# Attention with a gated MLP on one core: layernorm rstd of three row chunks by a power on GpSimd

## The chip, the cores and the metric

One core of one Trainium2 chip runs the whole kernel in one launch. Its engines are TensorE (PE in the profile, its weight loads PEld), VectorE (DVE), ScalarE (ACT), GpSimd (POOL) and SyncE (SP, which only issues DMAs here). They run side by side and wait for each other on semaphores; each executes its own instructions in order. The metric is the time of one execution in device microseconds, the median of the runs.

## The reference

The input x is 2048 rows of 448 numbers in bf16. A layernorm without weights feeds two branches whose product is added to x.

```python
def _layernorm(x, axis=-1, eps=1e-5):
    m = jnp.mean(x, axis=axis, keepdims=True)
    v = jnp.var(x, axis=axis, keepdims=True)
    return (x - m) / jnp.sqrt(v + eps)
...
    # branch A: H = 16 heads of Dh = 28
    qkv = (x @ wqkv).reshape(B, S, 3, H, Dh)...
    p = _softmax(einsum("bhqd,bhkd->bhqk", q, k) * Dh ** -0.5)
    s = einsum("bhqk,bhkd->bhqd", p, v).reshape(B, S, D) @ wo
    # branch B: F = 1792
    g = silu(gelu(x @ w1 + b1) @ w2 + b2)
...
    xn = _layernorm(x)
    return x + s * g
```

The number 1 / sqrt(v + eps) of each row is called rstd below.

## The kernel before

**Chunks and blocks.** The 2048 rows are four chunks c of 512 rows, each of four tiles t of 128 rows. The 16 heads are four groups g of four heads. One block b of attention is one group with one chunk of queries, 16 blocks in all, b = 4g + c. Within a block the scores of 16 key tiles and four heads are made 512 queries wide: 64 steps m. The scores of two steps (first block) or three (later) form a unit; the exponentials of a unit are one ACT instruction (L1038), numbered from 0 here. The scores come from PE (L1011) into a ring of PSUM banks. Since a step's key tile is its number over four, the first block meets the keys of chunk 1 at exponential 8, those of chunk 2 at exponential 16 and those of chunk 3 at exponential 24. Some steps, a fixed list, have their exponential on DVE instead (L1065 to L1096). The products with the values (L1137) follow on PE.

**Layernorm.** p_ln makes each chunk's mean and variance on DVE (L606, L612, into mv), for chunks 0 and 1 in two halves of two tiles, for chunks 2 and 3 four tiles at once. p_ln2 then makes rstd: on ACT a Ln of the variance with eps as bias (L620, into lnv) and an Exp with scale -0.5 (L622, into rstd). For chunk 0 DVE normalizes (L633). For chunks 1 to 3 POOL negates the mean (L627, nm) and normalizes each tile (L637). So before the change each half of chunk 1, and chunk 2 and chunk 3, has two small ACT instructions.

**From there to the scores.** PE transposes the normalized tiles (L651; chunk 0 L744), DVE copies them out (L662, into xnT), PE projects keys (L671) and DVE evicts them (L682, kT); the values go by L876 and L886, the queries by L671, L852, a square on POOL (L857), a sum on PE (L859) and L862.

**POOL's other early work.** It makes the constants (L496 to L534), two memsets of the value pads (L540, L541), and after the last chunk's layernorm the squares and relayouts of the query and key weights (L702, L692) and a memset of wo (L588). The 16 loads of wo on SP's queue wait for that memset; the norms (L804) wait for the squares.

**What else is named.** The first layer of branch B goes by L916 and L929. One Gelu per chunk (L941) runs on ACT in one stretch once all of them are done, between two loads of activation tables. The second layer is L959 (14 matmuls for one tile, two per task) and L964, and the silu a tanh on ACT (L973). The output is a matmul (L1226), a product and a sum (L1235, L1237) and a DMA.

**What sets the order.** The Python program works the order out when it builds the kernel. Every piece of work is a generator that yields tasks; a task has an engine, the tokens it reads and writes, a planned duration and a priority (`_Task(E, fn, reads, writes, dur, lat, prio)`). The loop in `run` takes, again and again, the task with the earliest planned start; among tasks of that engine that could start within 0.1 of it, the one with the smallest priority number goes first. It then books the task's planned duration. The planned durations are the program's own figures and not measurements. A task that reads what the one before it on its engine wrote waits for that engine's own semaphore (on all engines but PE), and its planned start is at least 0.07 later. So the booked order of every engine follows from planned starts, and the chip then executes that order, each engine in its own.

Of the kernel before, what the change touches and what calls it, by code (L numbers as in the profile page):

```python
# [7 lines left out]
ACTF = mybir.ActivationFunctionType  # L8
ALU = mybir.AluOpType
ET = mybir.EngineType  # L10

PE, ACT, DVE, POOL, SP = ET.PE, ET.Activation, ET.DVE, ET.Pool, ET.SP
# [55 lines left out]
LN_EPS = 1e-5  # L68
# [28 lines left out]
class _Kernel:  # L97
# [19 lines left out]
    def sb(self, name, shape, dtype=dt.bfloat16):  # L117
        return self.es.enter_context(self.nc.sbuf_tensor(name, shape, dtype))
# [143 lines left out]
    def alloc(self):  # L262
        nc = self.nc
        f32, bf = dt.float32, dt.bfloat16
        sb = self.sb
# [35 lines left out]
        self.rhi = sb("rhi", [128, 16, 32], bf)  # L301
        self.rlo = sb("rlo", [128, 16, 32], bf)
        self.dum = sb("dum", [128, 1], f32)
        self.epsc = sb("epsc", [128, 1], f32)
        w1f = self.w1[:, :, :].rearrange("p k f -> p (k f)")
        self.fsb = w1f[:, 0:3584].rearrange("p (b t d) -> p b t d", b=2, t=4)
# [159 lines left out]
    def constants(self):  # L466
        K = self
        e = self.emit

        def f(eng):  # L470
            eng.memset(K.epsc[:, :], LN_EPS)
            eng.memset(K.dum[:, :], 1.0)
            eng.memset(K.ones[:, :], 1.0)
            eng.memset(K.E_sb[:, :, :], 0.0)
            eng.memset(K.stg[64:128, 3, :, :, :], 0.0)
            pad = lambda w: w.rearrange("p k (h e) -> p (k h) e", e=32)[:, :, DH:32]
            eng.memset(pad(K.wq[:, :, :]), 0.0)
            eng.memset(pad(K.wk[:, :, :]), 0.0)
            eng.memset(pad(K.wsq), 0.0)
            return eng.memset(K.xn[:, :, :, D:512], 0.0)  # L480
        e(DVE, f, writes=[K.b_pads], dur=1.6)

        def late_pads():
            yield ("until", lambda: K.b_xnT[0][1].tw is not None)

            def f(eng):
                eng.memset(K.wv[64:128, 3, :], 0.0)
                eng.memset(K.wv[0:64, 3, D:WS], 0.0)
                return eng.memset(K.wv[:, 0:3, D:WS], 0.0)
            yield _Task(DVE, f, [], [K.b_wvpad], 0.4, 0.05, 1)  # L490
            yield ("until", lambda: K.ln_done == 2 * C)
            yield _Task(DVE, lambda eng: eng.memset(K.w1[64:128, 3, :], 0.0), [], [K.b_w1pad], 0.8, 0.05, 4)
        K.spawn(late_pads(), 3)

        def f(eng):
            eng.iota(K.iota_p[:, :], [[0, 1]], base=0, channel_multiplier=1, allow_small_or_imprecise_dtypes=True)  # L496
            return eng.iota(K.iota_f[:, :], [[1, 128]], base=0, channel_multiplier=0, allow_small_or_imprecise_dtypes=True)
        io = _Buf()
        e(POOL, f, writes=[io], dur=0.4)

        def f(eng):
            return eng.tensor_scalar(K.ident[:, :], K.iota_f[:, :], K.iota_p[:, 0:1], None, op0=ALU.is_equal)
        e(POOL, f, reads=[io], writes=[K.b_id], dur=0.6)
        ec, tc = _Buf(), _Buf()
        e(POOL, lambda eng: eng.tensor_copy(K.ecol[:, 0:1], K.iota_p[:, :]), reads=[io], writes=[ec], dur=0.2)
        for thr in (32.0, 64.0, 96.0):
            e(POOL, lambda eng, thr=thr: eng.tensor_scalar(K.tcol[:, :], K.iota_p[:, :], thr, 32.0,
                                                           op0=ALU.is_ge, op1=ALU.mult), reads=[io], writes=[tc], dur=0.3)
            e(POOL, lambda eng: eng.tensor_tensor(K.ecol[:, 0:1], K.ecol[:, 0:1], K.tcol[:, :], ALU.subtract),
              reads=[ec, tc], writes=[ec], dur=0.3)  # L510

        def f(eng):
            eng.tensor_single_scalar(K.ecol[:, 1:2], K.ecol[:, 0:1], 28.0, ALU.is_lt)
            eng.tensor_scalar(K.ecol[:, 2:3], K.ecol[:, 0:1], 28.0, -1.0, op0=ALU.is_equal, op1=ALU.mult)
            return eng.tensor_tensor(K.ecol[:, 3:4], K.iota_p[:, :], K.ecol[:, 0:1], ALU.subtract)
        e(POOL, f, reads=[ec, io], writes=[K.b_cols], dur=0.8)
        e(POOL, lambda eng: eng.tensor_scalar(K.tcol[:, :], K.ecol[:, 3:4], 28.0, None, op0=ALU.add),
          reads=[K.b_cols], writes=[tc], dur=0.3)
        hm = _Buf()

        def f(eng):
            return eng.tensor_scalar(K.ecol[:, 0:1], K.ecol[:, 1:2], 0.5, None, op0=ALU.mult)
        e(POOL, f, reads=[K.b_cols], writes=[hm], dur=0.3)

        def f(eng):
            return eng.tensor_scalar(K.bsel[:, :], K.iota_f[:, :], K.tcol[:, 0:1], K.ecol[:, 0:1],
                                     op0=ALU.is_equal, op1=ALU.mult)
        e(POOL, f, reads=[tc, hm, io], writes=[K.b_bsel], dur=0.8)

        def f(eng):  # L530
            return eng.tensor_copy(K.sel[:, :], K.ident[:, :].rearrange("p (j e) -> p j e", e=32)[:, :, DH])
        e(POOL, f, reads=[K.b_id], writes=[K.b_bsel], dur=0.2)
        selb = K.selb[:, :].rearrange("p (j e) -> p j e", e=32)
        e(POOL, lambda eng: eng.tensor_copy(selb, K.sel[:, :, None].to_broadcast([128, 4, 32])), reads=[K.b_bsel],  # L534
          writes=[K.b_selb], dur=0.3)
        K.b_hf[1][0].r.append(K.b_bsel.w)

        def vpads():
            yield ("until", lambda: K.ready(K.b_xn[0], -0.1))
            yield _Task(POOL, lambda eng: eng.memset(K.vaug[:, :, :, DH:DH + 1], 2.0), K.b_xn[0], [K.b_vpad0], 1.2, 0.05, 2)  # L540
            yield _Task(POOL, lambda eng: eng.memset(K.vaug[:, :, :, DH + 1:32], 0.0), [K.b_vpad0], [K.b_vpad], 1.2, 0.05, 2)  # L541
        K.spawn(vpads(), 3)
        self.prog[ACT].append(lambda eng: eng.preload_act_table_set("natural_log_exp_and_others"))
        self.tE[ACT] = 2.1
# [72 lines left out]
    def p_ln2(self, c, h, ts):  # L617
        K = self
        sl = slice(4 * c + ts[0], 4 * c + ts[-1] + 1)
        yield _Task(ACT, lambda eng: eng.activation(K.lnv[:, sl], K.mv[:, sl, 1], ACTF.Ln, bias=K.epsc[:, 0:1]),  # L620
                    [K.b_mv[c][h], K.b_pads], [K.b_ln[c][h]], 0.3, 0.0, 2 if c else 0)
        yield _Task(ACT, lambda eng: eng.activation(K.rstd[:, sl], K.lnv[:, sl], ACTF.Exp, scale=-0.5),  # L622
                    [K.b_ln[c][h]], [K.b_rs[c][h]], 0.2, 0.0, 2 if c else 0)
        if len(ts) == 4:
            K.b_rs[c][1] = K.b_rs[c][0]
        if c > 0:
            yield _Task(POOL, lambda eng: eng.tensor_scalar(K.nm[:, sl], K.mv[:, sl, 0], -1.0, None, op0=ALU.mult),  # L627
                        [K.b_mv[c][h]], [K.b_nm[c][h]], 0.22, 0.05, c)
        for t in ts:
            i = 4 * c + t  # L630
            rd = [K.b_x0[h] if c == 0 else K.b_x[c], K.b_mv[c][h], K.b_rs[c][h], K.b_pads]
            if c == 0:
                yield _Task(DVE, lambda eng, i=i, t=t: eng.tensor_scalar(  # L633
                    K.xn[:, c % 3, t, 0:D], K.x_sb[:, c, t, :], K.mv[:, i, 0:1], K.rstd[:, i:i + 1],
                    op0=ALU.subtract, op1=ALU.mult), rd, [K.b_xn[c % 3][t]], 0.38, 0.05, c)
            else:
                yield _Task(POOL, lambda eng, i=i, t=t: eng.tensor_scalar(  # L637
                    K.xn[:, c % 3, t, 0:D], K.x_sb[:, c, t, :], K.nm[:, i:i + 1], K.rstd[:, i:i + 1],
                    op0=ALU.add, op1=ALU.mult), rd + [K.b_nm[c][h]], [K.b_xn[c % 3][t]], 0.7, 0.05, c)
        K.ln_done += len(ts) // 2  # L640
# [676 lines left out]
```

## Time and profile before

| what | value |
|---|---|
| median of 5 runs | 499.01 us (496.51 to 499.98) |
| profiled execution | 497.67 us |
| its span | 495.9 us |
| granted TensorE clock, mean | 0.965 |
| ACT busy | 474.7 us (96%) |
| PE busy | 422.6 us (85%) |
| DVE busy | 388.1 us (78%) |
| POOL busy | 83.7 us (17%) |
| L620, six instructions | 287 to 297 ns each |
| L622, six instructions | 203 to 206 ns each |
| L627, four instructions | 228 to 239 ns each |
| L637, twelve instructions | 712 to 716 ns each |

The span runs from the first to the last instruction in the trace; the profiled execution took 1.77 us more. The profile's page gives the busy time of each engine and the groups of instructions by line; a group's row ends with the idle time of the engine just before its instructions and with what ended most of it. The timeline lists instructions in order of time with their start, their length and, in brackets, the idle time before them and the releaser. Idle time of an engine matters only where the work that comes later is on the path to the end.

### The profile page before, as it was taken

What the parts mean: (1) busy time and instruction counts of PE and PEld (TensorE: products, weight loads), DVE (VectorE), ACT (ScalarE), POOL (GpSimd) and SP (SyncE); (2) the same over time, 40 slices, a digit from 0 to 9 for tenths busy, and PEclk for the clock granted to TensorE, in tenths of its full rate; (3) what the DMA queues carried; (4) which work ended last, traced back from release to release, by engine and by line L of the source; (5) the groups of instructions that cost most, each with busy time, mean ns of one, the idle gap of its engine ahead of it and who ended that gap; (6) DMA issues with size and microseconds to landing.
All of it is one profiled execution on the core that took longest, in us unless ns stands there. A gap on an engine that the chain in (4) does not pass through costs nothing.

```text
span 495.9 us, 8658 instructions
## 1 busy us (share of the span) xinstructions
PE 422.6 (85%) x3519; PEld 140.2 (28%) x3519; DVE 388.1 (78%) x545; ACT 474.7 (96%) x382; POOL 83.7 (17%) x91
## 2 busy tenths in 40 slices
PE   6999889887988888888888888756999999998884
PEld 4442223221222222222222222111333333322442
DVE  7745998888698959997887969992297999678454
ACT  5999999999999999999999999999699999999994
POOL 6571112041210212121101020040000102010100
PEclk9999999998899999999999999975799999999998
DMA  8500000000000000002200000000001001102110
GB/s 240 147 16 21 0 1 1 0 1 2 1 1 1 0 1 0 2 1 62 69 1 0 1 1 1 1 0 0 1 1 38 2 0 38 38 0 75 40 49 30
DMA packets 10089, 11.00 MB, mean 22 GB/s; under 512 B 3457, under 2 KB 8705, under 8 KB 10049
## 3 DMA queue, kind: packets, MB, share of 16 engines
q1 hardware_dynamic: 9904, 10.21, 6.9%
q8 instruction: 28, 0.46, 0.4%
q10 hardware_dynamic: 144, 0.23, 0.1%
q14 instruction: 13, 0.10, 0.1%
HBM read 8.61 MB, written 1.84 MB: 21 GB/s over the span
## 4 chain that ended last, share of the span: by engine, by line
ACT 33%; PE 33%; issue 18%; DVE 12%; POOL 3%; DMA 1%; ACTq 0%; DVEq 0%; POOLq 0%
ACT P L1038 32%; PE ring L1011 8%; PE misc L959 7%; PE acc L1137 5%; PE misc L916 5%; PE misc L671 3%; DVE h L929 1%; POOL rlo L1202 1%; DVE x_sb L1065 1%; DVE kT L1090 1%; POOL rhi L1201 1%; ACT w L973 1%; PE misc L1226 1%; DVE x_sb L1096 1%; DVE kT L682 1%
## 5 line engine op out<-in xcount | busy, mean ns | idle before, releaser
L1038 ACT ACTIVATE P<-ring 128x1536 bf16<-128x1536 f32 (+1 forms) x352 | 434.6, 1448 | 8.6 <-PE ring L1011 7.8
L1011 PE MATMUL ring<-qT,kT 32*128 32x512 bf16 (+1 forms) x1216 | 137.6, 351 | 41.9 <-ACT P L1038 37.5
L1137 PE MATMUL acc<-P,vaug 128*32 128x512 bf16 (+1 forms) x1151 | 96.1, 353 | 0.7 <-ACT P L1038 0.4
L1011 PEld LDWEIGHTS ring<-qT,kT 32*128 32x128 bf16 x1216 | 36.9, 91 | 160.6 <-ACT P L1038 142.8
L916 PE MATMUL misc<-xnT,w 128*128 128x512 bf16 x224 | 62.8, 387 | 1.4 <-DVE qT L1216 0.4
L929 DVE TENSOR_SCALAR h<-misc,b1c 128x512 bf16<-128x512 f32 x56 | 41.8, 747 | 20.6 <-PE misc L916 20.2
L959 PE MATMUL misc<-w,h 128*128 128x448 bf16 x224 | 54.3, 369 | 2.0 <-DVE qT L852 0.9
L1201 POOL CAST rhi<-rc 128x512 bf16<-128x512 f32 x15 | 15.3, 1017 | 239.8 <-DVE rc L1197 215.4
L1065 DVE TENSOR_SCALAR x_sb<-ring 128x512 int32<-128x512 f32 x65 | 44.6, 687 | 7.8 <-PE ring L1011 7.5
L857 POOL TENSOR_TENSOR qsq<-qT 128x512 bf16<-128x512 bf16 x15 | 23.3, 1555 | 131.1 <-DVE qT L852 131.1
L1137 PEld LDWEIGHTS acc<-P,vaug 128*32 128x32 bf16 x1151 | 25.4, 94 | 55.8 <-issue 49.4
L959 PEld LDWEIGHTS misc<-w,h 128*128 128x128 bf16 x224 | 18.1, 100 | 27.9 <-issue 14.6
L941 ACT ACTIVATE h<-h 128x7168 bf16<-128x7168 bf16 x4 | 24.4, 6164 | 0.0
L916 PEld LDWEIGHTS misc<-xnT,w 128*128 128x128 bf16 x224 | 15.6, 98 | 29.8 <-issue 13.2
L671 PE MATMUL misc<-xnT,wq 128*128 128x512 bf16 x60 | 19.8, 447 | 3.9 <-DVE qT L862 2.1
L1202 POOL TENSOR_TENSOR rlo<-rc,rhi 128x512 bf16<-128x512 f32 x15 | 22.0, 1470 | 1.2
L1094 DVE SCALAR_TENSOR_TENSOR kT<-kT 128x1024 f32<-128x1024 f32 (+1 forms) x17 | 21.7, 1279 | 0.2
L964 DVE TENSOR_TENSOR w<-misc,b2b 128x448 bf16<-128x448 f32 x16 | 10.0, 622 | 15.2 <-PE misc L959 15.1
L1090 DVE SCALAR_TENSOR_TENSOR kT<-kT 128x1024 f32<-128x1024 f32 (+1 forms) x17 | 21.2, 1250 | 0.4
L1092 DVE SCALAR_TENSOR_TENSOR w<-w 128x1024 f32<-128x1024 f32 (+1 forms) x18 | 21.2, 1180 | 0.2
L1090 DVE SCALAR_TENSOR_TENSOR w<-w 128x1024 f32<-128x1024 f32 (+1 forms) x18 | 20.6, 1145 | 0.4
L1094 DVE SCALAR_TENSOR_TENSOR w<-w 128x1024 f32<-128x1024 f32 (+1 forms) x18 | 20.8, 1154 | 0.1
(135 smaller groups left out, 413.0 us busy)
## 6 DMA issues: line engine op xcount, KB each, us to landing
h<-in_A_x_dram SPq DMA_DIRECT2D x4, 448.0 KB, 3.3
w<-in_B_w_dram SPq DMA_DIRECT2D x1, 1568.0 KB, 7.3
x_sb<-in_A_x_dram SPq DMA_DIRECT2D x3, 448.0 KB, 5.8
w<-in_B_w_dram SPq DMA_DIRECT2D x1, 1344.0 KB, 7.5
out_dram<-h SPq DMA_DIRECT2D x6, 224.0 KB, 1.9
h<-in_A_wqkv_dram SPq DMA_DIRECT2D x3, 168.0 KB, 5.7
out_dram<-h SPq DMA_DIRECT2D x4, 112.0 KB, 1.7
wo<-in_A_wo_dram SPq DMA_DIRECT2D x16, 24.5 KB
```

Source lines behind the costliest of these rows:

```text
L671: ins = eng.matmul(bank, w[:, kt, g * 128:(g + 1) * 128], K.xnT[:, kt, c * 512:(c + 1) * 512], start=(kt == 0), stop=(kt == KT - 1))
L916: ins = eng.matmul(bank, K.w1[:, kt, ft * 128:(ft + 1) * 128], K.xnT[:, kt, c * 512:(c + 1) * 512], start=(kt == 0), stop=(kt == KT - 1))
L929: yield _Task(DVE, lambda eng: eng.tensor_scalar(dst, bank, K.b1c[:, ft:ft + 1], None, op0=ALU.add), [tok, K.b_b1c], wr, 0.75, 0.0, 2)
L941: return eng.activation(hv, hv, ACTF.Gelu_apprx_tanh)
L959: ins = eng.matmul(ps, hv[:, ft, t * 128:(t + 1) * 128], K.w2[:, ft, :], start=(ft == 0), stop=(ft == FT - 1))
L1011: return eng.matmul(K.ring[:, RB[m], col:col + nq], K.kT[32 * j:32 * j + 32, g, t * 128:(t + 1) * 128], K.qT[32 * j:32 * j + 32, g, c * 51 ...
L1038: return eng.activation(K.P[:, p0:p0 + n, :], K.ring[:, b0:b0 + n, :], ACTF.Exp, scale=SM_SCALE)
L1065: yield _Task(DVE, lambda eng, m=m, i=i, half=half: eng.tensor_scalar(K.ysb[i][:, 512 * half:512 * half + 512], K.ring[:, RB[m], :], SM_SC ...
L1090: yield _Task(DVE, lambda eng: eng.scalar_tensor_tensor(u, v, EXP_A, v, op0=ALU.add, op1=ALU.mult), [tv], [tu], d1, 0.0, 4)
L1094: yield _Task(DVE, lambda eng: eng.scalar_tensor_tensor(u, v, EXP_D, u, op0=ALU.mult, op1=ALU.add), [tv, tu], [tu], d1, 0.0, 4)
L1137: return eng.matmul(K.acc[32 * j:32 * j + 32, q0:q0 + nq], K.vaug[:, t, 4 * g + j, :], ap[:, col:col + nq], tile_position=(0, 32 * j), sta ...
L1202: yield _Task(En, lambda eng: eng.tensor_tensor(K.rlo[:, :, :], rcb, K.rhi[:, :, :], ALU.subtract), [K.b_rc, K.b_rhl], [K.b_rhl], d2, 0.0, 1)
```

## The change

For chunk 0 nothing changes. For chunks 1 to 3 the two ACT instructions are replaced by two on POOL: an addition of eps to the variance, and a two-input operation that raises it to a column of -0.5, broadcast over the tiles. The column is a new 128x1 tensor, mhalf, that DVE sets among its first memsets; the task of these memsets is the token b_pads, which the power waits for. The planned durations of the new tasks are 0.22 for the addition and 0.3 + 0.16 times the number of tiles for the power, 0.62 or 0.94. Their priority number is that of POOL's other layernorm tasks, the chunk's number. They come before nm in the generator's order.

```diff
+        self.mhalf = sb("mhalf", [128, 1], f32)
...
             eng.memset(K.epsc[:, :], LN_EPS)
+            eng.memset(K.mhalf[:, :], -0.5)
...
-        yield _Task(ACT, lambda eng: eng.activation(K.lnv[:, sl], K.mv[:, sl, 1], ACTF.Ln, bias=K.epsc[:, 0:1]),
-                    [K.b_mv[c][h], K.b_pads], [K.b_ln[c][h]], 0.3, 0.0, 2 if c else 0)
-        yield _Task(ACT, lambda eng: eng.activation(K.rstd[:, sl], K.lnv[:, sl], ACTF.Exp, scale=-0.5),
-                    [K.b_ln[c][h]], [K.b_rs[c][h]], 0.2, 0.0, 2 if c else 0)
+        if c == 0:
+            yield _Task(ACT, lambda eng: eng.activation(K.lnv[:, sl], K.mv[:, sl, 1], ACTF.Ln, bias=K.epsc[:, 0:1]),
+                        [K.b_mv[c][h], K.b_pads], [K.b_ln[c][h]], 0.3, 0.0, 0)
+            yield _Task(ACT, lambda eng: eng.activation(K.rstd[:, sl], K.lnv[:, sl], ACTF.Exp, scale=-0.5),
+                        [K.b_ln[c][h]], [K.b_rs[c][h]], 0.2, 0.0, 0)
+        else:
+            yield _Task(POOL, lambda eng: eng.tensor_scalar(K.lnv[:, sl], K.mv[:, sl, 1], LN_EPS, None, op0=ALU.add),
+                        [K.b_mv[c][h]], [K.b_ln[c][h]], 0.22, 0.05, c)
+            yield _Task(POOL, lambda eng: eng.tensor_tensor(K.rstd[:, sl], K.lnv[:, sl],
+                                                            K.mhalf[:, 0:1].to_broadcast([128, len(ts)]), ALU.pow),
+                        [K.b_ln[c][h], K.b_pads], [K.b_rs[c][h]], 0.3 + 0.16 * len(ts), 0.05, c)
```

## The prediction

> **What bounds the kernel now.** I read the page first: busy shares, then the costliest groups.
>
> ```profile
> span 495.9 us, 8658 instructions
> ...
> PE 422.6 (85%) x3519; PEld 140.2 (28%) x3519; DVE 388.1 (78%) x545; ACT 474.7 (96%) x382; POOL 83.7 (17%) x91
> ...
> L1038 ACT ACTIVATE P<-ring 128x1536 bf16<-128x1536 f32 (+1 forms) x352 | 434.6, 1448 | 8.6 <-PE ring L1011 7.8
> ```
>
> The softmax exponentials (L1038) fill ScalarE (ACT): 434.6 of 495.9 us, and all the waiting in front of them is 8.6 us. GpSimd (POOL) is busy 17%. A us taken from ACT is a us of span, but only where the next exponential already has its scores. So I read the timeline of ACT around the eight instructions that go (L620 and L622 of chunks 1 to 3). Columns: start, length, engine, line, count, and the idle time before it.
>
> ```profile
> 10.37 0.29 ACT L620 ACTIVATE lnv<-mv,epsc 128x2 f32<-128x2 f32 x1 [0.28 <-DVE mv L612]
> 10.70 0.20 ACT L622 ACTIVATE rstd<-lnv 128x2 f32<-128x2 f32 x1
> 10.94 0.60 ACT L769 ACTIVATE qsq<-ring 128x512 bf16<-128x512 f32 x1
> ...
> 12.41 0.29 ACT L620 ACTIVATE lnv<-mv,epsc 128x2 f32<-128x2 f32 x1
> 12.73 0.20 ACT L622 ACTIVATE rstd<-lnv 128x2 f32<-128x2 f32 x1
> 13.40 6.57 ACT L1038 ACTIVATE P<-ring 128x1024 bf16<-128x1024 f32 x7 [0.47 <-PE ring L1011]
> 19.87 0.29 ACT L620 ACTIVATE lnv<-mv,epsc 128x4 f32<-128x4 f32 x1
> 20.19 0.20 ACT L622 ACTIVATE rstd<-lnv 128x4 f32<-128x4 f32 x1
> 20.30 1.92 ACT L1038 ACTIVATE P<-ring 128x1024 bf16<-128x1024 f32 x2
> 22.11 0.30 ACT L620 ACTIVATE lnv<-mv,epsc 128x4 f32<-128x4 f32 x1
> 22.43 0.21 ACT L622 ACTIVATE rstd<-lnv 128x4 f32<-128x4 f32 x1
> 22.55 6.52 ACT L1038 ACTIVATE P<-ring 128x1024 bf16<-128x1024 f32 x7
> 29.81 15.27 ACT L1038 ACTIVATE P<-ring 128x1024 bf16<-128x1024 f32 x16 [0.75 <-PE ring L1011]
> ```
>
> Two pairs stand ahead of the first exponential, two inside the stream. The stream stops at 29.07 for 0.75 us: exponential 16 (counted from 0) is the first that needs the keys of chunk 2, and the timeline of VectorE (DVE) has that key eviction (L682) at 28.57 to 29.32.
>
> **What is removed.** Pair at 10.37: the square behind it reads a projection whose last matmuls (L671) run 10.31 to 10.90, so it starts at 10.9 anyway: 0. Pair at 12.41: the first exponential waits for score matmuls at 12.97 to 13.37: 0. Pair at 19.87: seven exponentials take 6.57, one alone 1.03 (the 17 of this form in 8 to 30 us average 1031 ns), so they start every (6.57 - 1.03)/6 = 0.92; number 7 would start at 13.40 + 7 x 0.92 = 19.86, not 20.30: 0.44. Pair at 22.11: likewise about 0.44. Together 0.88 us of ACT, half of what eight instructions suggest. Whether any of it stays depends on the keys, and they come through POOL.
>
> **What is added.** One 128x1 memset on DVE at the start: 0.03 to 0.04 us by the neighbours' start spacing (0.80, 0.84, 0.87). DVE then idles 0.83 us for the first x transfer: 0; without that cover 0.04. On POOL, per half of chunk 1 and per chunk 2 and 3, an add and a power in the same order as these:
>
> ```profile
> 9.90 1.23 POOL L541 MEMSET vaug<- 128x768 bf16 x1
> 11.03 0.24 POOL L627 TENSOR_SCALAR nm<-mv 128x2 f32<-128x2 f32 x1
> 11.47 1.42 POOL L637 TENSOR_SCALAR h<-x_sb,nm,rstd 128x448 bf16<-128x448 bf16 x2 [0.20 <-POOL nm L627]
> 12.86 0.23 POOL L627 TENSOR_SCALAR nm<-mv 128x2 f32<-128x2 f32 x1
> 13.26 1.41 POOL L637 TENSOR_SCALAR h<-x_sb,nm,rstd 128x448 bf16<-128x448 bf16 x2 [0.17 <-POOL nm L627]
> 18.49 0.23 POOL L627 TENSOR_SCALAR nm<-mv 128x4 f32<-128x4 f32 x1 [3.83 <-DVE mv L612]
> 20.55 2.80 POOL L637 TENSOR_SCALAR h<-x_sb,nm,rstd 128x448 bf16<-128x448 bf16 x4 [1.83 <-ACT rstd L622]
> ```
>
> The add is like L627: 0.23, then 0.17 until a dependent instruction starts, so 0.40. No row shows a power. Below, a two-input 128x1 operation (L509) takes 0.19; above, the longest POOL instruction of the early timeline (L702, 128x1344) takes 2.43. The diff's planning figures are 0.62 (two columns) and 0.94 (four); its figures for L627 and L637 (0.22, 0.70) agree with their rows (0.23, 0.71), so I take 0.62 and 0.94 and keep both ends (another of its figures is off: L1201 is planned at 0.62 and reads 1.02 in the mean).
>
> [...] In this trace the first add, copy and compare on POOL follow each other with at most 0.15 us between them; no row shows a power. [...]
>
> *Chunk 1.* Its rstd is ready at 10.90 today, but POOL is in the memset until 11.03, so the wait for ACT was hidden: the new work is all added. Each half gains 0.40 + 0.62 = 1.0; the second half's add may slip into the first half's wait, so the last normalized tile moves from 14.67 to between 16.2 and 16.7; I take 16.5, +1.8. Its keys were evicted at 18.62 to 19.37, 4.70 after; of that some 1.0 is PE queueing (transposes 0.62, copy 0.7, projection 1.04 and eviction 0.75, plus the second transpose and copy, need about 3.7). New: 20.2 to 21.2. Exponential 8, the first to need them, ran at 21.2 and could now run at 20.8; its scores take 0.4 after the keys, so it runs at 20.8 to 21.65. The late end eats nearly all of the 0.88: exponential 9 then starts at 22.57, against 22.55 before.
>
> *Chunk 2.* Statistics end at 18.40 on DVE. POOL finished nm at 18.72 and waited until 20.55, because rstd stood behind seven exponentials on ACT. New: add 18.46, power 18.86 to 19.80, nm to 20.23, tiles 20.23 to 23.03 instead of 20.55 to 23.35: 0.32 earlier. From here to the keys PE is full (7.74 of 7.74 us in the stretch 21.36 to 29.10), so they come at most 0.32 earlier, and so does exponential 16: 29.5 instead of 29.81. ACT itself could be there by 29.1 or sooner; what is late next is this eviction. So 0.3 us is won.
>
> *Chunk 3.* POOL reaches it after chunk 2's tiles: add at 23.0, tiles 24.8 to 27.6, +1.0. Its keys end at 32.74 before, 33.7 then; exponential 24 needs them at 29.5 + 8 x 0.95 = 37.1: covered by 3.4. The weight relayouts (L702, L692) and the memset of wo behind them move +1.0, and so do wo's 16 loads on SP's queue, which wait for that memset; the first user of the relayouts I see is the norm matmul at 41.09, and wo is first read with the output. Covered.
>
> **Sum.** From 29.81 sixteen exponentials run without a gap, so 0.3 us is carried to the end. Bounds: at power 0.19, chunk 2 is 1.05 earlier and exponential 8 not later than before, -1.05. At 2.43, chunk 1's last tile ends near 19.95, its keys at 23.7 to 24.7, exponential 8 at 24.1 to 25.1, exponential 16 eight spacings later at 31.5 to 32.5: +1.7 to +2.7. The profiled execution took 497.67 (span 495.9 and 1.77 around it); with -0.3, 497.4. It lies 1.34 under the median of the five runs, 499.01; I predict against the median: 498.7. By 0.5% (2.5 us) a measurement of this kernel can be told from no change; this can't.
>
> **What the sum does not hold.** The order on all engines is worked out by a greedy list from planned starts. Shift a few early ones and later choices may fall otherwise, for all 480 us. ACT's own work stays the same, so what can change is its idle time: after 30 us there are gaps of 0.58, 0.29, 1.07, 3.69, 0.80 and 0.18 us. The big one stands behind Gelu:
>
> ```profile
> 346.81 2.37 ACT L1038 ACTIVATE P<-ring 128x1024 bf16<-128x1024 f32 x2
> 352.86 2.54 ACT L1038 ACTIVATE P<-ring 128x1536 bf16<-128x1536 f32 x2 [3.69 <-PE ring L1011]
> ```
>
> PE runs 14 second-layer matmuls (L959) at 347.16 to 352.48, 380 ns each, at a granted clock of 0.64 over 320 to 353 us; six of them at 354.51 take 1.31 together, 0.22 each. The next scores (L1011) are queued behind them, at 352.42.
>
> **Rivals.**
> 1. *Slower: a worse order after Gelu.* If the new list puts a second tile of 14 matmuls in front of those scores, ACT waits 14 x 0.22 to 0.38 = 3.1 to 5.3 us more, 4.2 in the middle: 498.7 + 4.2 = 502.9. It decides from some 8 to 13 matmuls more, 2.8 us. For it: whichever work is left for that place changes with the list. Against: the queue of work is spawned in the same order. 0.28.
> 2. *Slower: power on POOL is the bound.* Even 2.43 us gives at most 501.7; it takes about 2.5 us and more to be told apart. at 4 us the two halves of chunk 1 add 2 x 1.6 more, some 504. For it: no row shows the operation. Against: the diff's figures. 0.05.
> 3. *Faster: a better order after Gelu.* The scores go ahead of the matmuls and the 3.69 goes: 498.7 - 3.7 = 495.0. 0.22.
> 4. *It does nothing:* ACT's 0.88 turns into waiting for chunk 1's and chunk 2's keys, 499.0. 0.09.
>
> **How the numbers follow.** The forecast, 498.7, has 0.36; its own range with the bounds of the power is 497.9 to 501.4. Within 0.5%: 0.36 + 0.09 = 0.45. Slower: 0.28 + 0.05 = 0.33. Faster: 0.22. The range reaches to both order rivals, 494.5 to 504.0.
>
> **What would show it.** ACT has no Ln after 8 us; the power's row reads near 0.6 and 0.9 us; chunk 1's tiles end near 16.5, chunk 2's near 23.0; exponential 8 starts near 21.5 and exponential 16 near 29.5. The gap after Gelu tells which order rival, if any, holds. I am wrong if the power takes over 2.5 us, if chunk 2's keys do not follow its tiles, or if the gaps after 30 us differ from 6.6 us in sum by more than 2.5.

## The result, and the profile after

The changed kernel takes 500.97 us (median of 44 runs, 498.87 to 506.07); the kernel before, run beside it, 498.98 us (79 runs, 495.89 to 501.16). The ratio is 1.0052, with a 95% interval of 1.0039 to 1.0065: slower by about 2.6 us, where 0.3 us faster was forecast. The ratio compares means; the medians differ by 2.0 us, because 16 of the 44 runs took over 502 us, and none of the 79 runs of before did. The ratios in this document leave out two runs that were over 1.5% above the fastest of their kernel: 505.56 us of e4_chunk1 and 1079.62 us of e2_new_order_ln, the last of which nothing on record explains.

The profiled execution took 500.04 us. The page's span, engine shares and largest group, as shown of before:

```profile
span 498.2 us, 8668 instructions
...
PE 422.5 (85%) x3518; PEld 139.4 (28%) x3518; DVE 388.0 (78%) x546; ACT 473.5 (95%) x374; POOL 90.4 (18%) x99
...
L1047 ACT ACTIVATE P<-ring 128x1536 bf16<-128x1536 f32 (+1 forms) x352 | 434.9, 1448 | 11.9 <-PE ring L1020 11.1
```

ACT has its eight instructions fewer, and the exponentials (now L1047) take as long as before. But the idle time in front of them grew from 8.6 to 11.9 us, and scores (now L1020) ended most of it. The timeline of ACT shows where the early part of it lies (3.1 us up to exponential 16, against 1.2 in the same rows of before):

```profile
13.18 3.77 ACT L1047 ACTIVATE P<-ring 128x1024 bf16<-128x1024 f32 x4 [0.88 <-PE ring L1020]
17.90 3.77 ACT L1047 ACTIVATE P<-ring 128x1024 bf16<-128x1024 f32 x4 [0.95 <-PE ring L1020]
22.16 7.44 ACT L1047 ACTIVATE P<-ring 128x1024 bf16<-128x1024 f32 x8 [0.49 <-PE ring L1020]
30.39 15.23 ACT L1047 ACTIVATE P<-ring 128x1024 bf16<-128x1024 f32 x16 [0.78 <-PE ring L1020]
```

No Ln is left among them. Besides the gaps before the first exponential and before exponential 16, which before has too, there are two new ones, before exponential 4 (0.95 us) and exponential 8 (0.49). Counted from the first exponential, so that the start does not matter, exponential 16 comes at 30.39 - 13.18 = 17.21 us; before it was 29.81 - 13.40 = 16.41. So 0.8 us is lost by then, although 0.9 us of work was taken away.

Exponential 4 needs only keys of chunk 0. Why its scores were late is in PE's timeline (L660 are the transposes of chunk 1; they come after the scores of exponential 3):

```profile
15.17 0.39 PE L1020 MATMUL ring<-qT,kT 32*128 32x512 bf16 x2
15.49 0.40 PE L660 MATMUL misc<-ident,h 128*128 128x128 bf16 x4
17.16 0.38 PE L660 MATMUL misc<-ident,h 128*128 128x128 bf16 x4 [1.27 <-POOL h L646]
17.47 0.39 PE L1020 MATMUL ring<-qT,kT 32*128 32x512 bf16 x2
```

The transposes of chunk 1's second half stand ahead of the scores of exponential 4 in PE's queue. PE stood still for 1.27 us until POOL's tiles (L646) were there, with the scores of exponential 4 behind, which wait for nothing of chunk 1. Before, with the tiles there at 14.67, the same transposes (L651) and the scores behind them ran without a wait:

```profile
14.80 0.62 PE L651 MATMUL misc<-ident,h 128*128 128x128 bf16 x8
15.39 0.39 PE L1011 MATMUL ring<-qT,kT 32*128 32x512 bf16 x2
```

POOL's timeline, second half of chunk 1, add, power, nm and two tiles:

```profile
14.06 0.22 POOL L628 TENSOR_SCALAR lnv<-mv 128x2 f32<-128x2 f32 x1
14.37 0.72 POOL L630 TENSOR_TENSOR rstd<-lnv,mhalf 128x2 f32<-128x2 f32 x1
15.17 0.25 POOL L636 TENSOR_SCALAR nm<-mv 128x2 f32<-128x2 f32 x1
15.60 1.41 POOL L646 TENSOR_SCALAR h<-x_sb,nm,rstd 128x448 bf16<-128x448 bf16 x2 [0.18 <-POOL nm L636]
```

The last tile ends at 17.01, against 14.67 before. The power takes 0.72 us for two columns (planned 0.62) and 1.04 for four (0.94).

### The profile page after: what moved, and what is told of

It is laid out like the page before. It is cut to its first block, busy times and chain, and to the rows that moved or that the text cites. A ratio compares the mean times of both kernels' runs of the same rounds, so it can differ in the third digit from the quotient of the medians.

```text
span 498.2 us, 8668 instructions
## 1 busy us (share of the span) xinstructions
PE 422.5 (85%) x3518; PEld 139.4 (28%) x3518; DVE 388.0 (78%) x546; ACT 473.5 (95%) x374; POOL 90.4 (18%) x99
## 4 chain that ended last, share of the span: by engine, by line
ACT 36%; PE 34%; issue 15%; DVE 11%; POOL 3%; DMA 1%; ACTq 0%; POOLq 0%; DVEq 0%
ACT P L1047 35%; PE ring L1020 9%; PE misc L968 7%; PE misc L925 6%; PE acc L1146 6%; PE misc L680 3%; DVE h L938 2%; POOL h L646 1%; DVE x_sb L1074 1%; DVE qT L871 1%; ACT w L982 1%; PE misc L1235 1%; DVE kT L1099 1%; DVE x_sb L1105 1%; PE ring L680 1%
## 5 line engine op out<-in xcount | busy, mean ns | idle before, releaser
L1047 ACT ACTIVATE P<-ring 128x1536 bf16<-128x1536 f32 (+1 forms) x352 | 434.9, 1448 | 11.9 <-PE ring L1020 11.1
L1020 PE MATMUL ring<-qT,kT 32*128 32x512 bf16 (+1 forms) x1216 | 137.6, 352 | 42.9 <-ACT P L1047 38.1
L1146 PE MATMUL acc<-P,vaug 128*32 128x512 bf16 (+1 forms) x1151 | 95.2, 354 | 0.6 <-ACT P L1047 0.2
L1020 PEld LDWEIGHTS ring<-qT,kT 32*128 32x128 bf16 x1216 | 36.8, 91 | 164.4 <-ACT P L1047 147.6
L925 PE MATMUL misc<-xnT,w 128*128 128x512 bf16 x224 | 64.0, 391 | 2.4 <-DVE qT L1225 0.8
L1146 PEld LDWEIGHTS acc<-P,vaug 128*32 128x32 bf16 x1151 | 24.9, 94 | 54.0 <-issue 48.1
L1211 POOL TENSOR_TENSOR rlo<-rc,rhi 128x512 bf16<-128x512 f32 x15 | 23.1, 1539 | 1.2
L680 PE MATMUL misc<-xnT,wq 128*128 128x512 bf16 x56 | 18.4, 452 | 4.4 <-DVE qT L871 2.7
L1103 DVE SCALAR_TENSOR_TENSOR w<-w 128x1024 f32<-128x1024 f32 (+1 forms) x18 | 21.8, 1211 | 0.1
L1099 DVE SCALAR_TENSOR_TENSOR kT<-kT 128x1024 f32<-128x1024 f32 (+1 forms) x17 | 20.8, 1224 | 0.4
L1103 DVE SCALAR_TENSOR_TENSOR kT<-kT 128x1024 f32<-128x1024 f32 (+1 forms) x17 | 20.9, 1228 | 0.2
L1099 DVE SCALAR_TENSOR_TENSOR w<-w 128x1024 f32<-128x1024 f32 (+1 forms) x18 | 20.6, 1145 | 0.3
L1105 DVE SCALAR_TENSOR_TENSOR x_sb<-x_sb,kT 128x1024 uint16<-128x1024 int32 (+1 forms) x17 | 20.5, 1205 | 0.2
```

What stands on the lines that cost most here:

```text
L680: ins = eng.matmul(bank, w[:, kt, g * 128:(g + 1) * 128], K.xnT[:, kt, c * 512:(c + 1) * 512], start=(kt == 0), stop=(kt == KT - 1))
L925: ins = eng.matmul(bank, K.w1[:, kt, ft * 128:(ft + 1) * 128], K.xnT[:, kt, c * 512:(c + 1) * 512], start=(kt == 0), stop=(kt == KT - 1))
L1020: return eng.matmul(K.ring[:, RB[m], col:col + nq], K.kT[32 * j:32 * j + 32, g, t * 128:(t + 1) * 128], K.qT[32 * j:32 * j + 32, g, c * 51 ...
L1047: return eng.activation(K.P[:, p0:p0 + n, :], K.ring[:, b0:b0 + n, :], ACTF.Exp, scale=SM_SCALE)
L1099: yield _Task(DVE, lambda eng: eng.scalar_tensor_tensor(u, v, EXP_A, v, op0=ALU.add, op1=ALU.mult), [tv], [tu], d1, 0.0, 4)
L1103: yield _Task(DVE, lambda eng: eng.scalar_tensor_tensor(u, v, EXP_D, u, op0=ALU.mult, op1=ALU.add), [tv, tu], [tu], d1, 0.0, 4)
```

## The experiments

Theory A: the loss comes from this wait in PE's queue. Theory B: it comes from the new order as such, wherever the power runs. In the first two kernels the place where a task is booked and the engine that executes it are separated, so that the order of all engines stays exactly that of one kernel while the rstd is made as in the other.

**Old order, power on POOL** (e1_old_order_pow): `_Task` gets an executing engine `em`.

```diff
+            yield _Task(ACT, lambda eng: eng.tensor_scalar(K.lnv[:, sl], K.mv[:, sl, 1], LN_EPS, None, op0=ALU.add),
+                        [K.b_mv[c][h], K.b_pads], [K.b_ln[c][h]], 0.3, 0.0, 2, em=POOL)
+            yield _Task(ACT, lambda eng: eng.tensor_tensor(K.rstd[:, sl], K.lnv[:, sl], ..., ALU.pow),
+                        [K.b_ln[c][h]], [K.b_rs[c][h]], 0.2, 0.0, 2, em=POOL)
```

> The order of every engine is that of before; only the rstd of chunks 1 to 3 is made by add and power on POOL instead of ACT. Theory A (TensorE's queue is held up: transposes of chunk 1 stand ahead of scores and wait for POOL's later tiles): the old order has these transposes even earlier (14.8 us), so they wait until about 17.0, exponential 3 and what follows starts some 2 us late, exponential 16 some 1 to 1.5 us later than in before (29.81), and the time is 500.0 to 501.0. Theory B (what costs is the new order that the list makes, wherever the power runs): near before, 498.7 to 499.3.

507.38 us (6 runs; before beside it 499.12), ratio 1.0170 (1.0125 to 1.0215). Slower as A has it, but by 8 us instead of 1 to 2: exponential 16 starts only at 40.00:

```profile
40.00 15.27 ACT L1048 ACTIVATE P<-ring 128x1024 bf16<-128x1024 f32 x16 [1.54 <-PE ring L1021]
```

The table by stretches tells what A lacked (columns: stretch, length, busy time of PE, PEld, DVE, ACT and POOL, then granted TensorE clock, DMA share, GB/s):

```profile
15.00:18.00 3.00, 0.84 (x10) 0.44 (x8) 0.78 (x3) 1.34 (x2) 2.03 (x4) 1.00 0.89 189
18.00:21.00 3.00, 2.67 (x18) 1.19 (x18) 2.59 (x8) 2.81 (x3) 0.14 (x1) 0.68 0.97 331
21.00:24.00 3.00, 3.00 (x16) 1.17 (x15) 1.28 (x2) 1.18 (x3) 2.62 (x5) 0.50 0.17 48
24.00:27.00 3.00, 3.00 (x17) 1.37 (x15) 1.54 (x6) 1.97 (x2) 1.33 (x4) 0.50 0.00 0
```

PE waits 2.16 us for POOL here and is busy 0.84 of 3 us; 1.6 us after the end of that wait its granted clock is halved, and it stays so from 19.1 to 39.6 us. From 21 us on PE is busy 3.00 of 3 us in these rows while ACT waits, so the whole stage goes by the slower PE.

**New order, Ln and Exp on ACT** (e2_new_order_ln):

```diff
+            yield _Task(POOL, lambda eng: eng.activation(K.lnv[:, sl], K.mv[:, sl, 1], ACTF.Ln, bias=K.epsc[:, 0:1]),
+                        [K.b_mv[c][h]], [K.b_ln[c][h]], 0.22, 0.05, c, em=ACT)
+            yield _Task(POOL, lambda eng: eng.activation(K.rstd[:, sl], K.lnv[:, sl], ACTF.Exp, scale=-0.5),
+                        [K.b_ln[c][h], K.b_pads], [K.b_rs[c][h]], 0.3 + 0.16 * len(ts), 0.05, c, em=ACT)
```

> The order of every engine is that of the changed kernel; the rstd of chunks 1 to 3 is made by Ln and Exp on ACT, put in the order at the places of the add and the power. Theory A: chunk 1's tiles are ready by about 15, no wait of TensorE for POOL at the transposes, the gap of 0.95 us before exponential 4 goes, ACT pays 0.9 us for the two pairs in its stream; 499.0 to 500.0. Theory B: as slow as the changed kernel, 501, with gaps between 100 and 165 us that add up to about 2.6.

499.00 us, ratio 0.9996 (0.9970 to 1.0023). The new order alone costs nothing that can be measured. Exponential 16 comes at 29.63 - 13.45 = 16.18 after the first. Theory B falls.

```profile
13.45 6.52 ACT L1047 ACTIVATE P<-ring 128x1024 bf16<-128x1024 f32 x7 [0.39 <-PE ring L1020]
29.63 15.23 ACT L1047 ACTIVATE P<-ring 128x1024 bf16<-128x1024 f32 x16 [0.43 <-PE ring L1020]
```

**The parts of the change**: chunks 2 and 3 alone (e3_chunks23), `if c < 2` instead of `if c == 0` ahead of the ACT tasks; chunk 1 alone (e4_chunk1), `if c != 1`.

> The power on POOL for chunks 2 and 3 alone; chunk 1 keeps Ln and Exp on ACT. Theory A: chunk 1's tiles end near 14.7 as in before, no wait at the transposes, two pairs leave the stream of exponentials: exponential 16 no later than in before, 498.3 to 499.2. Theory B: the list is a new one again, so up to 2 us either way, no link with the early part.

> The power on POOL for chunk 1 alone; chunks 2 and 3 keep Ln and Exp on ACT. Theory A: all of the early loss is here: chunk 1's tiles end near 17.0, a gap of about 1 us before exponential 4 or 5, exponential 16 at 30.4 or later; 500.5 to 502. Theory B: no more than by chance, 498 to 501.

Chunks 2 and 3: 499.04 us, ratio 1.0002 (0.9981 to 1.0022). Chunk 1: 501.91 us, ratio 1.0045 (1.0016 to 1.0074), 6 of 12 runs over 502. So the loss is chunk 1's. In the trace of the chunk-1 kernel PE waits 1.22 us at the same transposes, and the clock is 0.62 from 17 to 19 us and 0.50 from 19 to 23; in that of the changed kernel, after 1.27 us, it stayed at 1.00. The six traces further below show why.

With chunks 2 and 3 the stream does run through (16 exponentials without a gap), and stops at the point that the prediction names, the keys of chunk 2:

```profile
13.44 14.82 ACT L1047 ACTIVATE P<-ring 128x1024 bf16<-128x1024 f32 x16 [0.47 <-PE ring L1020]
29.45 15.44 ACT L1047 ACTIVATE P<-ring 128x1024 bf16<-128x1024 f32 x16 [1.19 <-PE ring L1020]
```

The 0.9 us taken from ACT are there, and 0.44 of it became waiting (1.19 instead of 0.75). Counted from the first, exponential 16 is 0.40 earlier than before, too little to be seen in the time.

**A later plan for chunk 1** (e6_late_plan), no other instruction:

```diff
-                        [K.b_ln[c][h], K.b_pads], [K.b_rs[c][h]], 0.3 + 0.16 * len(ts), 0.05, c)
+                        [K.b_ln[c][h], K.b_pads], [K.b_rs[c][h]], (1.4 if c == 1 else 0.3 + 0.16 * len(ts)), 0.05, c)
```

> The changed kernel with a planned duration of 1.4 instead of 0.62 for the power of chunk 1; no instruction differs, only the order that the list makes. The plan then has chunk 1's second transposes behind the scores of exponential 5, near 17.3 on the chip, when the tiles are there (17.0). Theory A: TensorE's wait of 1.27 us for POOL is under 0.3, the gap before exponential 4 goes, but chunk 1's keys come no earlier, so a gap of about 1 us before exponential 8 takes its place: exponential 16 within 0.5 of 30.4, time 500 to 501.5. Theory B: any order may turn out 1 to 2 us better or worse after 46 us.

500.05 us, ratio 1.0029 (1.0005 to 1.0052), no run of 12 over 502. The wait moved as expected, from exponential 4 to exponential 8, where the keys of chunk 1 are needed:

```profile
13.49 7.44 ACT L1047 ACTIVATE P<-ring 128x1024 bf16<-128x1024 f32 x8 [0.81 <-PE ring L1020]
22.22 1.94 ACT L1047 ACTIVATE P<-ring 128x1024 bf16<-128x1024 f32 x2 [1.29 <-PE ring L1020]
25.07 21.09 ACT L1047 ACTIVATE P<-ring 128x1024 bf16<-128x1024 f32 x22 [0.91 <-PE acc L1146]
```

A second gap that was not expected, 0.91 us before exponential 10, ends on a product with the values (L1146). At the even pace of the last row exponential 16 comes near 17.3 after the first, 0.9 later than in before. So here too the later tiles cost about 1 us. What goes is the part that comes and goes from run to run.

**The pairs left out** (e7_no_rstd), old order, the rstd of chunks 1 to 3 not computed (constants in its place):

```diff
+            yield _Task(ACT, lambda eng: eng.memset(K.rstd[:, sl], 20.0),
+                        [K.b_ln[c][h]], [K.b_rs[c][h]], 0.2, 0.0, 2, em=DVE)
```

> The order of before with the four Ln and Exp pairs of chunks 1 to 3 left out, nothing on POOL: their rstd is not computed, two small DVE memsets write constants in its place. Both theories: the four pairs are worth what the first estimate says, 0.3 to 0.9 us, because two pairs stand in ACT's idle time: 498.1 to 498.7, exponential 16 at 29.0 to 29.6. If it is under 497.5 the pairs were worth more than their time on ACT.

498.18 us (before beside it 498.87), ratio 0.9983 (0.9958 to 1.0008); exponential 16 at 29.62 - 13.50 = 16.12 after the first, 0.3 earlier. That is about what the removal can give with the old order, and the interval does not part it from nothing.

**Theory C**: besides the direct 0.8 us, PE's wait halves its clock for several us in some of the runs. If so, keeping PE busy in the wait must take these runs away. Theory D: the slow runs have another cause. In the changed kernel (e8_after_fill), the old order with the power (e9_old_order_pow_fill, 20 instead of 12) and chunk 1 alone (e14_chunk1_fill), matmuls whose result nobody reads were put ahead of the transposes:

```diff
         for h in range(2):
+            if c == 1 and pr == 0 and h == 1:
+                for _ in range(12):
+                    K.prog[PE].append(lambda eng: eng.matmul(K.acc[:, 0:256], K.ident[:, :], K.E_sb[:, 0, 0:256],
+                                                             start=True, stop=True))
             yield K.t_tr(c, pr, h, bank, tok, 1.5)
```

> The changed kernel with 12 idle-filling matmuls (256 columns, result unused) on TensorE ahead of the transposes of chunk 1's second half, so that TensorE works through most of its 1.27 us wait for POOL; everything else is the same. Theory C (the wait itself costs about 1 us, and in some runs TensorE's clock is halved for 5 to 20 us after it, as the traces of the chunk-1-only and old-order kernels show): no run over 502.5, clock at least 0.955 in nearly all runs, median 499.8 to 500.3. Theory D (the slow runs have another cause): the same spread as the changed kernel, a quarter of the runs over 502.5.

> The old order with the power on POOL for chunks 1 to 3 (507.4 us), with 20 such matmuls ahead of the same transposes, about 2.1 us of work in the 2.16 us wait. Theory C: granted clock stays 1.00 between 18 and 38 us, exponential 16 starts at 31.5 to 33 instead of 40.0, time 500 to 502. Theory D: 505 or more.

> The power on POOL for chunk 1 alone (501.9 us, 6 of 12 runs over 502), with 12 idle-filling matmuls on TensorE ahead of the transposes of chunk 1's second half, as in the changed kernel with fillers. Theory C: no run over 502, clock 1.00 between 17 and 25 us, median 499.0 to 500.3. Theory D: half of the runs over 502 again.

The changed kernel with them takes 498.87 us (before beside it 499.13), ratio 0.9999 (0.9980 to 1.0019); none of 12 runs is over 500.4, and the median is 0.9 us under the range that theory C gave. The old order with the power falls from 507.38 to 501.47, ratio 1.0054 (1.0033 to 1.0074). Chunk 1 alone goes from 501.91 to 500.31, ratio 1.0027 (1.0004 to 1.0049), with one run of 12 over 502 instead of six, where theory C had none. The stretches of the old order with fillers, to be read beside those without:

```profile
15.00:18.00 3.00, 3.00 (x30) 2.29 (x28) 0.76 (x3) 1.32 (x2) 2.03 (x4) 1.00 0.74 134
18.00:21.00 3.00, 3.00 (x24) 1.27 (x23) 2.82 (x9) 2.81 (x4) 0.14 (x1) 1.00 1.01 382
21.00:24.00 3.00, 3.00 (x32) 1.67 (x30) 2.50 (x8) 3.00 (x5) 2.63 (x5) 1.00 0.26 66
```

The transposes start at 17.45 in both, so the fillers shorten no wait. Yet exponential 16 comes at 32.73 instead of 40.00:

```profile
32.73 15.27 ACT L1052 ACTIVATE P<-ring 128x1024 bf16<-128x1024 f32 x16 [0.75 <-PE ring L1025]
```

The 7.3 us between them go with the clock, which stays at 1.00 here; the rest, 32.73 against 29.81, is the direct price of the old order.

**Six more traces of the changed kernel** (e11_after_again, e12_after_look, e13_after_look, e15_after_look, e16_after_look, e17_after_look): the same kernel, one profiled execution each, to find one with a halved clock.

> The changed kernel once more, one look. Theory C: if this run is over 502, its trace has a granted clock near 0.5 after 17 us and exponential 16 later than 32; if it is under 501, the clock there is 1.00 and exponential 16 near 30.4.

> The changed kernel, one more look, since 16 of its 44 runs were over 502 us and neither trace so far is of such a run. Theory C: a run over 502 has a granted clock near 0.5 for several us from about 17 us on, exponential 16 later than 31.5; a run under 501.5 has 1.00 there and exponential 16 about 17.2 after the first.

> The same as the look before: over 502 with the clock near 0.5 after 17 us, or under 501.5 with 1.00.

> The changed kernel, one look, in search of a run over 502: theory C has the clock near 0.5 for some us after 17 us in such a run, and 1.00 there in a run under 501.5.

> The changed kernel, a second look: theory C has the clock near 0.5 for some us after 17 us if the run is over 502, and 1.00 there if it is under 501.5.

> The changed kernel, a third look: theory C has the clock near 0.5 for some us after 17 us if the run is over 502, and 1.00 there if it is under 501.5.

They took 500.25, 500.22, 501.29, 500.12, 505.19 and 500.00 us. The one over 502 has what theory C asks for. Its ACT timeline and its stretches:

```profile
13.41 3.77 ACT L1047 ACTIVATE P<-ring 128x1024 bf16<-128x1024 f32 x4 [0.89 <-PE ring L1020]
18.24 1.02 ACT L1047 ACTIVATE P<-ring 128x1024 bf16<-128x1024 f32 x1 [1.06 <-PE ring L1020]
19.75 2.10 ACT L1047 ACTIVATE P<-ring 128x1024 bf16<-128x1024 f32 x2 [0.48 <-PE ring L1020]
22.55 1.02 ACT L1047 ACTIVATE P<-ring 128x1024 bf16<-128x1024 f32 x1 [0.70 <-PE ring L1020]
25.37 7.44 ACT L1047 ACTIVATE P<-ring 128x1024 bf16<-128x1024 f32 x8 [1.80 <-PE ring L1020]
33.23 15.22 ACT L1047 ACTIVATE P<-ring 128x1024 bf16<-128x1024 f32 x16 [0.42 <-PE ring L1020]
```

```profile
15.00:17.00 2.00, 1.03 (x9) 0.35 (x7) 1.63 (x4) 2.00 (x3) 1.73 (x4) 1.00 0.81 241
17.00:19.00 2.00, 1.61 (x14) 1.10 (x14) 0.69 (x1) 0.94 (x2) 0.24 (x1) 0.71 1.03 413
19.00:21.00 2.00, 2.00 (x10) 0.56 (x9) 1.76 (x7) 1.46 (x3) 0.65 (x2) 0.50 0.52 152
21.00:23.00 2.00, 2.00 (x7) 0.45 (x6) 0.36 (x1) 1.30 (x2) 1.71 (x4) 0.50 0.00 2
23.00:25.00 2.00, 2.00 (x22) 1.63 (x19) 1.04 (x5) 0.57 (x1) 1.97 (x3) 0.58 0.00 0
25.00:27.00 2.00, 1.65 (x22) 0.47 (x23) 0.62 (x1) 1.63 (x2) 1.52 (x3) 1.00 0.00 0
```

PE's wait is 1.26 us, against 1.27 in the first profile, but the clock is halved from 17.9 to 24.7 us, and the gap before exponential 8 is 1.80 us instead of 0.49. Exponential 16 comes 19.82 after the first, 2.6 later than in the first profile.

Theory C was wrong in one thing: it tied the halving to times over 502. The executions of 501.29 and 500.00 us have it too (exponential 16 at 20.5 and 19.2 after the first). They win part back later: from the table load after Gelu to the exponentials behind the gap they take 6.24 us each, the first profile 7.29, the one of 505.19 us 8.15. So of the seven traces of the changed kernel three have the early halving and four don't, with 2.8 to 4.1 us lost at exponential 16 against 0.8, all counted from before's 16.41. That is a mean of 4/7 x 0.8 + 3/7 x 3.4 = 1.9 us at exponential 16, of the 2.6 between the mean times. No other trace shows a clock below 1.00 between 15 and 38 us, save those of the chunk-1 and old-order kernels without fillers, where PE also waits for POOL at these transposes.

What parts the traces with the halving from those with the same wait and no halving can be read from the times at which the clock changes. Every halved stretch that a trace holds whole lasts a multiple of 3.41 us: 6.83 from 17.86 to 24.68 in the trace above, 10.24 from 17.05 to 27.29 in that of 501.29 us, 20.48 from 19.08 to 39.56 in the old order with the power. The stretches at full clock between two halved ones do too: 6.83 and 201.39 us in before (2 and 59 times 3.413), 13.65, 23.89 and 174.08 in the first profile of the changed kernel (4, 7 and 51 times). So the clock changes on a grid of 3.41 us steps in these traces, and the grid lies elsewhere from one to the next: a step ends at 17.78 us in before, at 16.59 in the first profile, and at 17.86, 17.05 and 19.08 in the three named above. In the four traces of the changed kernel without the halving a step ends inside PE's wait, and no step holds more than 0.77 us of it; PE is busy 2.21 to 2.28 us of that step. In the three with the halving one step holds 0.89, 1.26 and 1.19 us of the wait (PE busy 2.09, 2.01 and 2.22), in the chunk-1 kernel 1.22 (2.01), in the old order with the power 1.79 (1.64), and the clock is halved from the end of that step on. With the fillers PE is busy 2.98 us or more of the steps that hold the place of the wait, and the clock stays. So the place of the grid, which differs from execution to execution, goes with the halving in all nine traces that have the wait; PE's busy time alone parts them only nearly (2.21 without, 2.22 with). No run varied that place by itself.

**The forecast without chunk 1** (e10_old_order_23): old order, power on POOL for chunks 2 and 3, chunk 1 on ACT; e1's tasks under `if c < 2` / `else`.

> The order of before on every engine; power on POOL for chunks 2 and 3 alone, chunk 1 on ACT. This is the forecast without what happened to chunk 1: chunk 2's tiles end near 23.0, two pairs leave ACT's stream, exponential 16 at 29.1 to 29.6 instead of 29.81, time 0.2 to 0.7 under before, 498.2 to 498.8. If it is at or over before, POOL's chain of chunk 2 costs something too.

499.59 us (before 499.13), ratio 1.0003 (0.9985 to 1.0022). Exponential 16 comes at 30.36 - 13.42 = 16.94 after the first, 0.5 later than before, where the prediction had 0.3 earlier. ACT's timeline at exponential 16 and POOL's for chunk 2:

```profile
30.36 15.27 ACT L1048 ACTIVATE P<-ring 128x1024 bf16<-128x1024 f32 x16 [0.75 <-PE ring L1021]
```

```profile
18.51 0.23 POOL L629 TENSOR_SCALAR lnv<-mv 128x4 f32<-128x4 f32 x1 [3.84 <-DVE mv L615]
18.83 1.04 POOL L631 TENSOR_TENSOR rstd<-lnv,mhalf 128x4 f32<-128x4 f32 x1
19.96 0.24 POOL L637 TENSOR_SCALAR nm<-mv 128x4 f32<-128x4 f32 x1
20.40 2.11 POOL L647 TENSOR_SCALAR h<-x_sb,nm,rstd 128x448 bf16<-128x448 bf16 x3 [0.20 <-POOL nm L637]
22.59 0.23 POOL L629 TENSOR_SCALAR lnv<-mv 128x4 f32<-128x4 f32 x1
22.81 0.71 POOL L647 TENSOR_SCALAR h<-x_sb,nm,rstd 128x448 bf16<-128x448 bf16 x1
```

The chain is 0.15 earlier, not 0.32, and chunk 3's add is booked ahead of the last tile, which ends at 23.52, later than before (23.35). PE waits 0.28 us for it, and 0.33 us more at 26.66 for chunk 3's first tiles, whose transposes stand ahead of chunk 2's key projection (L681 at 27.29). It is the same kind of wait as with chunk 1.

## Why the prediction was wrong

**ACT's 0.88 us**: right. With chunks 2 and 3 alone, 16 exponentials run without a gap where before two pairs stood in between. The two early pairs were put at nothing; the first exponential starts at 13.09 to 13.50 us in the traces without them and at 13.40 to 13.45 with them, so no gain is clear of the spread.

**The power's price**: 0.72 and 1.04 us where 0.62 and 0.94 were taken, far inside the bounds. The first power of the execution starts 0.32 us after the start of the add ahead of it and takes 0.73; the second has 0.31 and 0.72. Each half also has 0.08 us between the power and the next instruction, and the second half's add (14.06) did not slip into the first half's wait, so chunk 1's last tile ended at 17.01 instead of 16.5.

**The step that failed** is the one for chunk 1: "Exponential 8, the first to need them, ran at 21.2 and could now run at 20.8". It followed the late tiles to the keys and the keys to their first use, as if PE served whoever is ready. The first that the tiles held up was not their user but what stood behind them in PE's queue: the scores of exponential 4, which need nothing of chunk 1. PE stood still for 1.27 us there, ACT waited 0.95 us before exponential 4 and 0.49 before exponential 8, and exponential 8 ran at 22.16. The prediction had read that queue for chunk 2 ("PE is full") and not for chunk 1. The same delay went on through DVE's queue: chunk 2's statistics (L614, at 19.06 instead of 18.04) stand behind the copies of chunk 1's transposes, so POOL got them 1.0 us later and chunk 2's tiles ended at 24.21 instead of the 23.03 forecast. So 0.3 us earlier at exponential 16 became 0.8 later. DVE's rows, before and after, and POOL's tiles of chunk 2 after:

```profile
18.04 0.36 DVE L612 BATCH_NORM_AGGREGATE mv<-st 128x2 f32<-128x6 f32 x4
```

```profile
17.58 0.69 DVE L671 COPY xnT<-misc 128x1024 bf16<-128x1024 bf16 x1 [1.19 <-PE misc L660]
18.45 0.69 DVE L671 COPY xnT<-ring 128x1024 bf16<-128x1024 bf16 x1 [0.18 <-PE ring L660]
19.06 0.37 DVE L614 BATCH_NORM_AGGREGATE mv<-st 128x2 f32<-128x6 f32 x4
```

```profile
21.41 2.80 POOL L646 TENSOR_SCALAR h<-x_sb,nm,rstd 128x448 bf16<-128x448 bf16 x4 [0.20 <-POOL nm L636]
```

**What was missing** is the clock. The prediction read the granted clock only after Gelu, where it saw 0.64, and took the early stage at full clock. The trace of before shows 1.00 there, with PE busy 3.1 us in each of the two 3.41 us steps from 10.95 to 17.78; it could not show what a longer wait does. The bound of +1.7 to +2.7 us for a power of 2.43 us leaves this out as well: no run has such a power, but the old order with one of 0.72 already lost 8 us.

**The rivals.** No new order after Gelu decided anything: the wait there is 3.62 us in the first profile against 3.69, and it ranges from 2.58 to 4.50 over the seven traces of the changed kernel, which have one and the same order. The gaps after 30 us add up to 8.0 us in the first profile, against 6.6 in before. The 1.4 more lie between 46 and 162 us, beside clock halvings that fall elsewhere in each trace; how much of that follows from the early delay is not shown. "Power on POOL is the bound" had the right side and place, but was held to decide only from 2.5 us on. "It does nothing" is what chunks 2 and 3 do by themselves. That the measured time lies inside the range is luck: the range was made that wide by the order rivals, and the bound for the power reaches 500.97 only with a power far slower than the one measured. The end of that bound is also uneven, 501.7 under rival 2 and 501.4 in the range, where 2.7 is counted from 498.7 instead of 499.01.

**What stays open**: the changed kernel with fillers keeps the direct loss in its trace (exponential 16 at 17.26 after the first) and still has a median of 0.3 us under before. Its interval, -1.0 to +0.9 us, just holds the 0.8; whether later clock dips, which differ from run to run, make up for it was not tried. No version tried beats the kernel before beyond its interval.

## What to carry to other kernels

Before moving work to an idle engine, follow its result into the queues of the engines that use it, and ask what stands behind the first waiting instruction; here the price was paid there first, before the result's own user. Where TensorE bounds a stage, a wait of 1.2 to 1.3 us cost 2.0 to 3.3 us more by exponential 16 at a halved clock here, in some runs and not in others, so look at several traces and at the spread of the times. Idle-filling matmuls in front of the known wait took most of that part away (500.97 to 498.87 us, 507.38 to 501.47, 501.91 to 500.31), and the exponential behind the wait started at most 0.02 us later with them (4.73 us after the first against 4.72 in the changed kernel, 4.72 against 4.70 in the old order, 4.60 against 4.79 with chunk 1 alone).

## What the runs showed of the hardware

- Waits of 1.19 to 1.29 us, in a stretch where PE was busy 0.72 to 1.12 of 2 us (15 to 17 us), were followed by a halved clock in four of eight traces (three of seven of the changed kernel and the chunk-1 kernel's); a wait of 2.16 us in the one trace that has it, and all six runs of that kernel were over 504 us.
- The halved stretches last 3.41, 6.83, 10.24, 20.48 or 23.89 us in all traces, but for those that the end of a trace cuts off. In before the clock changes at 113.35, 116.77, 123.59, 127.01, 328.39 and 352.29 us, which are 1, 2, 1, 59 and 7 steps of 3.413 us apart; in the first profile of the changed kernel at 108.75, 112.16, 125.81, 129.23, 153.12, 156.53, 330.61 and 354.51, which are 1, 4, 1, 7, 1, 51 and 7 apart. The two grids are offset by 1.19 us.
- In the three traces of the changed kernel with the early halving, 0.89 to 1.26 us of PE's wait lay in one such step, and PE was idle 1.19 to 1.40 us of that step; in the four without it, at most 0.77, and PE was idle 1.13 to 1.20.
- The power on GpSimd takes 0.72 us for 128x2 and 1.04 for 128x4 numbers, some 0.16 more per column between these two.
